# One-bank PSUM tiles for the feed-forward part, in a pool that opens where the pool of the attention's score tiles closes

## The chip, the cores and the metric

The kernel runs on one core of a Trainium2 chip, as one program in one launch. The metric is the time of an execution in microseconds of the device; where several executions are given, their median stands for the kernel. A profile comes from one execution, and its times count from the first instruction of that execution.

## The reference

The reference computes attention and then two feed-forward layers, all in float32.

- Attention: two batches of eight heads, 576 positions, 64 columns a head. q and k are rotated by position, the scores are softmax(q k^T / 8), and the result is the scores times v.
- The result is laid out as 1152 tokens of 512 columns, x.
- First layer: h = max(x w_in, 0) with 2048 columns, and y = (h * h) w_out, 512 columns.
- Second layer: a = y w_a and b = y w_b with 1536 columns each, and the output is (a * b) w2_out, 1152 x 512.

## The kernel before, in words

**How it is ordered.** The body of the kernel doesn't issue instructions as it goes. It describes operations to a planner (class `Plan`): which engines may run each, how long it is taken to last, which operations it follows, which buffers it takes (`acq`) and which it gives back (`rel`). `Plan.order` plays that forward in time and gives one list, and `Plan.run` then calls the operations' functions in the order of the list. For TensorE (PE), ScalarE (ACT), VectorE (DVE) and GpSimd (POOL) the framework keeps that order on each engine (`manual_schedule` at the end of the kernel function); SyncE (SP), which issues the DMAs, isn't in that list of engines. Which semaphore waits an instruction gets is not in the kernel's text: the framework works them out from the tiles that an instruction reads and writes.

**PSUM.** PSUM has eight banks of 512 float32 columns. One pool, `ps`, holds all of it in six tags: `s0` and `s1` of two banks each, and `t0`, `t1`, `u0`, `u1` of one bank each.

- In the attention, a score tile (`scores`, lines 334 to 370) is a tile of shape [128, 2, 512] on `s0` or `s1`. PE writes the two halves of a row of scores into its two banks, and DVE reads both banks at once (line 364) to negate them and take the row's extreme; ACT then takes the exponential. Transposes go to `t0`/`t1`, products with v and the sums' spreading to `u0`/`u1`.
- In the feed-forward part the planner knows six banks by name, `m0` to `m5` (`BANKS`, line 260). `m0` to `m3` are the two halves of two tiles of shape [128, 2, 512] on `s0` and `s1` (`SM`, line 258); `m4` and `m5` are one-bank tiles on `u0` and `u1` (`TM`, line 259; they appear as `mu` in the profile, the other four as `m`). `t0` and `t1` serve the conversion of weights there. Each of these feed-forward tiles is made when it is first used and stays to the end.
- The planner gives each bank out by itself: `bank` (line 513) asks for any of the six, takes the one that is free first, and the operation that reads it last gives it back. The four halves come free in the plan when the last scores are through.

**The feed-forward part.** The numbers are split into a high and a low part, so a product of two matrices takes three matmuls (`three`, lines 606 to 609: high by high, high by low, low by high).

- `unit1` (line 628): one block of 128 columns of h for 384 tokens, 12 matmuls of 384 columns into one bank. ACT takes the maximum with zero out of the bank (line 645), DVE multiplies that by the bank once more (line 646), then ACT and POOL or DVE split the square into its two parts (lines 520 and 517).
- `out1` (line 660): 12 matmuls into one bank, which ACT copies or DVE adds into an accumulator in SBUF (`yacc`, lines 654 and 655).
- `split_y`: the accumulated y is split, and sums and differences of its blocks are made for the second layer, which multiplies 2 x 2 blocks by seven products instead of eight.
- `super2` (line 728): seven products, each six matmuls of 288 columns, into three banks called al, be and gm; ACT copies out of them (lines 760, 764, 768), DVE adds and multiplies out of them (lines 772, 776, 781, 785).
- `out2` (line 799): six matmuls of 512 columns into one bank, which DVE adds into the output's accumulator (`oacc`, line 655); the last round's sums go to HBM by DMA (line 834).
- `convert` and `two_parts` turn weights, loaded as 8-byte numbers, into the two parts; ACT, DVE and POOL share that work, and it runs beside the matmuls all through the feed-forward part, until about 540 us.

In time, the last scores are written at about 147 us, the first `unit1` starts at 157.5 us, the second layer at about 360 us, and the last matmul ends at about 578 us.

Of the kernel before, what the change touches and what calls it, by code (L numbers as in the profile page):

```python
# [7 lines left out]
F32 = mybir.dt.float32  # L8
# [8 lines left out]
P = 128  # L17
# [14 lines left out]
NS = 2  # L32
# [189 lines left out]
def attention_moe_moe2_kernel(ctx: ExitStack, tc: tile.TileContext, qk, rope, vm, vt, ident_in, sel_in, w_in, w_out, w_a, w_b, w2_out, out):  # L222
# [3 lines left out]
    sb = ctx.enter_context(tc.tile_pool(name="sb", bufs=1))  # L226
    st_p = ctx.enter_context(tc.tile_pool(name="st", bufs=3))
    ps = ctx.enter_context(tc.tile_pool(name="ps", bufs=1, space=bass.MemoryType.PSUM))

    xall = sb.tile([P, 2, KC, NTB * TB], F32R, tag="x", name="x")  # L230
    CR = sb.tile([P, 2, 2, S], F32, tag="g2", name="cs_rot")
# [15 lines left out]
    def lazy(make):  # L247
        got = []

        def get():  # L250
            if not got:
                got.append(make())
            return got[0]
        return get

    WB = lazy(lambda: sb.tile([P, NWB, 2, DM], F32R, tag="wb", name="w_b"))
    STAGS, TTAGS, UTAGS = tuple(f"s{k}" for k in range(NS)), ("t0", "t1"), ("u0", "u1")
    SM = [lazy(lambda k=k: ps.tile([P, 2, 512], F32, tag=f"s{k}", name=f"m{k}")) for k in range(NS)]
    TM = [lazy(lambda t=t: ps.tile([P, 512], F32, tag=t, name=f"m{t}")) for t in UTAGS]
    BANKS = {f"m{k}": (lambda k=k: SM[k // 2]()[:, k % 2]) if k < 2 * NS else TM[k - 2 * NS] for k in range(2 * NS + 2)}  # L260
    MTAGS = tuple(BANKS)
    WTAGS = ("wa",) + tuple(f"wb{k}" for k in range(NWB))
    pl = Plan({
# [15 lines left out]
    def half(h):  # L279
        return slice(64 * h, 64 * h + 64)  # L280
# [31 lines left out]
    def rotate(p):  # L312
        b, rot = XA[p], ROT[p % 2]
        done = load_qk_done[p]
        war = [SDONE[p - 2, 4]] if p > 1 else []
        r = {}

        def x():
            return b()

        if p:
            for qi in (1, 0):
                m = pl.op("POOL", ("s", 2 * S), lambda e, qi=qi: e.tensor_tensor(out=x()[:, :, qi, :], in0=x()[:, :, qi, :], in1=cs, op=ALU.mult), [done[qi, 0]])  # L323
                r[qi] = pl.op("POOL", ("s", S), lambda e, qi=qi: e.tensor_tensor(out=rot[:, qi, :], in0=x()[:, 0, qi, :], in1=x()[:, 1, qi, :], op=ALU.add), [m] + war)
            r[2] = r[0]
        else:
            for key, qi, c in ((1, 1, slice(0, S)), (0, 0, slice(0, QS)), (2, 0, slice(QS, S))):
                w = c.stop - c.start
                m = [pl.op(FLEX, ("s", w), lambda e, n=n, qi=qi, c=c: e.tensor_tensor(out=x()[:, n, qi, c], in0=x()[:, n, qi, c], in1=cs[:, n, c], op=ALU.mult), [done[1, n] if qi else done[0, c.start]] + done[1, n].k0[:n + 1]) for n in range(2)]
                r[key] = pl.op(FLEX, ("s", w), lambda e, qi=qi, c=c: e.tensor_tensor(out=rot[:, qi, c], in0=x()[:, 0, qi, c], in1=x()[:, 1, qi, c], op=ALU.add), m)  # L330
        pl.op(None, None, None, list(r.values()), rel=[b])
        ROPE[p] = r

    def scores(p, c):
        rot = ROT[p % 2]
        if c == 0:
            rotate(p)
            ST[p] = lazy(lambda: st_p.tile([P, 2, 9], F32, tag="st", name=f"st{p}"))
        r = ROPE[p]
        tail = c == 4  # L340
        s = [Buf(STAGS, {t: (lambda t=t, h=h: ps.tile([P, 2, 512], F32, tag=t, name=f"s{p}_{c}_{h}")) for t in STAGS}) for h in range(1 if tail else 2)]
        SB[p, c] = s
        pr = Buf("P", None)
        pr.k = len(EXP) % NP
        st = ST[p]

        def mm(e):
            k0 = [rot[half(h), 1, :] for h in range(2)]
            if tail:
                q0 = (rot[half(0), 0, 512:576], rot[half(1), 0, 0:64])  # L350
                for h, bk, c0, kk, n in ((0, 0, 0, 0, 288), (1, 1, 0, 352, 224), (1, 1, 224, 0, 64), (0, 1, 0, 288, 288), (1, 0, 0, 64, 288)):
                    pe.matmul(s[0]()[half(h), bk, c0:c0 + n], q0[h], k0[h][:, kk:kk + n], start=True, stop=True, skip_group_check=True)  # L352
            else:
                for bk in range(2):
                    for h in range(2):
                        q0 = rot[half(h), 0, 64 * h + c * P:64 * h + (c + 1) * P]
                        pe.matmul(s[h]()[:, bk, 0:288], q0, k0[h][:, bk * 288:bk * 288 + 288], start=True, stop=True)  # L357

        o = pl.op("PE", ("us", 1.15), mm, [r[1], r[0]] + ([r[2]] if c else []), acq=s)
        SDONE[p, c] = o  # L360
        ex = []
        for h in range(len(s)):
            j = 2 * c + h
            m = pl.op("DVE", ("us", 0.85), lambda e, h=h, j=j: e.tensor_scalar(  # L364
                out=PP[:, pr.k, h, :].rearrange("p (b n) -> p b n", b=2), in0=s[h]()[:, :, 0:288], scalar1=-1.0, scalar2=None,
                op0=ALU.mult, op1=ALU.min, accum_out=st()[:, 0, j:j + 1]), [o], acq=[pr] if h == 0 else [], rel=[s[h]])
            x = pl.op("ACT", ("us", 0.86), lambda e, h=h, j=j: e.activation(  # L367
                PP[:, pr.k, h, :], PP[:, pr.k, h, :], AF.Exp,
                bias=st()[:, 0, j:j + 1], scale=-1.0, accum_out=st()[:, 1, j:j + 1]), [m])
            ex.append(x)  # L370
        EXP[p, c] = (pr, ex)
# [141 lines left out]
    def bank(name, width):  # L513
        return Buf(MTAGS, {t: (lambda f=f: f()[:, 0:width]) for t, f in BANKS.items()})

# [340 lines left out]
    fixed.append(dma(54, lambda e: e.dma_start(out=sel32, in_=sel_in)))  # L856
    zeros += [pl.op("POOL", ("us", 0.2), lambda e, t=t: e.memset(t, 0.0)) for t in VT]
    scores(0, 0)
    for n, (p, c) in enumerate(order):
        if n + 1 < len(order):  # L860
            scores(*order[n + 1])
        if c == 0:
            load_v(p)
        if c == 1 and 0 < p < NPAIR - 1:
            load_qk_done[p + 1] = load_qk(p + 1)
        if c == 4:
            if p:
                flip(p - 1)
            turned(p, c, 0)
            if p:  # L870
                spread(p - 1, 0)
            turned(p, c, 1)
            if p:
                spread(p - 1, 1)
            recip(p)
        else:
            turned(p, c, 0)
            turned(p, c, 1)
            if p:
                times_v(p - 1, c // 2, c % 2)  # L880
            if c == 3:
                turned(p, c, 2)
        if (p, c) == GATE:
            for k in range(3):
                wide.append(pl.op("DVE", ("us", 0.06), lambda e, k=k: e.memset(sb.tile([P, DM], I64, tag="raw", bufs=3, name=f"later{k}").bitcast(I32)[:, 0:1], 0), EXP[p, c][1]))
    p = NPAIR - 1
# [129 lines left out]
```

## Time and profile before

| what | value |
|---|---|
| median of 3 executions | 583.15 us (583.06 to 583.92) |
| the profiled execution | 583.75 us |
| its span, first to last instruction | 582.0 us |
| PE busy | 562.5 us (97%), 3554 matmuls |
| PE's weight loads | 486.7 us (84%) |
| DVE busy | 395.2 us (68%) |
| ACT busy | 326.9 us (56%) |
| POOL busy | 306.9 us (53%) |
| DMA | 51.16 MB, 88 GB/s on the mean |
| granted TensorE clock | 1.00 on the mean over the span |

The table is the profile's first page. Busy time is the time in which an engine had an instruction of its own under way. PE's matmuls are pipelined, so that one begins while the one before still drains: a matmul of 384 columns is shown with 0.33 us, though the next starts 0.17 us after it. An engine's idle time is listed with what ended it, the releaser: the instruction whose semaphore was the last to let the waiting one go. Tiles are named without their numbers: `m` is any of the four halves, `mu` either of the two one-bank tiles. A row of a timeline gives start, duration, engine, line, operation, out<-in, and in brackets the engine's idle time just before it with its releaser.

### The profile page before, as it was taken

What the parts mean: (1) busy time and instruction counts of PE and PEld (TensorE: products, weight loads), DVE (VectorE), ACT (ScalarE), POOL (GpSimd) and SP (SyncE); (2) the same over time, 40 slices, a digit from 0 to 9 for tenths busy, and PEclk for the clock granted to TensorE, in tenths of its full rate; (3) what the DMA queues carried; (4) which work ended last, traced back from release to release, by engine and by line L of the source; (5) the groups of instructions that cost most, each with busy time, mean ns of one, the idle gap of its engine ahead of it and who ended that gap; (6) DMA issues with size and microseconds to landing.
All of it is one profiled execution on the core that took longest, in us unless ns stands there. A gap on an engine that the chain in (4) does not pass through costs nothing.

```text
span 582.0 us, 9472 instructions
## 1 busy us (share of the span) xinstructions
PE 562.5 (97%) x3554; PEld 486.7 (84%) x3554; DVE 395.2 (68%) x748; ACT 326.9 (56%) x690; POOL 306.9 (53%) x260
## 2 busy tenths in 40 slices
PE   3999999999999999999999999999999999999997
PEld 2666666666699999999999999899988988988986
DVE  3646777776378736836764768987887877886454
ACT  1668888887478657705732545467753654534210
POOL 4598765421377505804761366776656666655000
PEclk9999999999999999999999999999999999999999
DMA  8326242120124423403330210213341322300004
GB/s 280 137 82 211 103 174 94 57 74 21 37 82 138 144 70 112 142 3 109 110 102 8 73 37 1 63 59 134 109 144 42 106 72 73 127 20 1 1 1 163
DMA packets 16018, 51.16 MB, mean 88 GB/s; under 512 B 2889, under 2 KB 3785, under 8 KB 15076
## 3 DMA queue, kind: packets, MB, share of 16 engines
q1 hardware_dynamic: 15972, 50.55, 25.7%
q8 instruction: 28, 0.46, 0.3%
q14 instruction: 18, 0.15, 0.1%
HBM read 48.19 MB, written 2.36 MB: 87 GB/s over the span
## 4 chain that ended last, share of the span: by engine, by line
PE 87%; DVE 7%; POOL 1%; ACT 1%; issue 1%; DMA 1%; SPq 0%; DVEq 0%; POOLq 0%; ACTq 0%
PE m L607 13%; PE m L609 12%; PE m L608 12%; PE s L357 7%; PE t L378 6%; PE av L436 6%; PE mu L607 5%; PE mu L608 5%; PE mu L609 5%; PE m L814 3%; PE m L816 2%; PE m L815 2%; PE av L438 2%; DVE oacc L655 1%; PE s L352 1%; PE mu L816 1%
## 5 line engine op out<-in xcount | busy, mean ns | idle before, releaser
L364 DVE TENSOR_SCALAR_CACHE_REDUCE P<-s 128x576 f32<-128x576 f32 x72 | 52.3, 755 | 32.7 <-PE s L357 24.5
L517 POOL TENSOR_TENSOR g<-v,g 128x384 fp32r<-128x384 f32 (+1 forms) x39 | 46.7, 1199 | 47.0 <-ACT g L520 46.8
L367 ACT ACTIVATE P<-P,st 128x576 f32<-128x576 f32 x72 | 55.5, 775 | 11.9 <-DVE P L364 11.9
L520 ACT CAST g<-v 128x384 fp32r<-128x384 f32 (+1 forms) x72 | 40.6, 566 | 28.2 <-DVE v L785 18.1
L607 PE MATMUL m<-y,w_p 128*128 128x288 f32 x160 | 48.1, 301 | 2.8 <-DVE v L772 1.8
L608 PE MATMUL m<-y,w_p 128*128 128x288 f32 x160 | 47.2, 295 | 0.0
L609 PE MATMUL m<-y,w_p 128*128 128x288 f32 x160 | 47.1, 294 | 0.0
L378 PEld LDWEIGHTS t<-small,P 128*128 128x128 f32 x288 | 31.4, 143 | 14.6 <-issue 10.6
L378 PE MATMUL t<-small,P 128*128 128x128 f32 x288 | 41.3, 285 | 0.0
L323 POOL TENSOR_TENSOR X<-X,cs_rot 128x1152 f32<-128x1152 f32 x14 | 36.7, 2635 | 1.1 <-DMA small<-in_sel 1.1
L607 PEld LDWEIGHTS m<-y,w_p 128*128 128x128 f32 x160 | 30.0, 187 | 6.4 <-DVE oacc L655 2.7
L607 PE MATMUL m<-x,w_i 128*128 128x384 f32 x100 | 33.7, 337 | 0.7 <-DVE v L646 0.5
L357 PE MATMUL s<-cs_rot 64*128 64x288 f32 x128 | 24.5, 484 | 9.8 <-POOL cs_rot L330 8.8
L609 PE MATMUL m<-x,w_i 128*128 128x384 f32 x100 | 33.4, 334 | 0.0
L608 PE MATMUL m<-x,w_i 128*128 128x384 f32 x100 | 33.4, 334 | 0.0
L760 ACT COPY v<-m 128x288 f32<-128x288 f32 x19 | 7.6, 400 | 42.0 <-PE m L609 26.7
L608 PEld LDWEIGHTS m<-y,w_p 128*128 128x128 f32 x160 | 30.1, 188 | 1.1
L517 POOL TENSOR_TENSOR w_i<-bits_i,w_i 128x512 fp32r<-128x512 f32 x8 | 10.3, 1282 | 39.2 <-ACT w_i L520 39.2
L609 PEld LDWEIGHTS m<-y,w_p 128*128 128x128 f32 x160 | 30.0, 188 | 0.0
L655 DVE TENSOR_TENSOR oacc<-m,oacc 128x512 f32<-128x512 f32 (+1 forms) x31 | 20.8, 678 | 12.7 <-PE m L816 7.7
L655 DVE TENSOR_TENSOR yacc<-m,yacc 128x384 f32<-128x384 f32 (+1 forms) x26 | 13.4, 517 | 22.9 <-PE m L609 22.6
L517 DVE TENSOR_TENSOR g<-v,g 128x384 fp32r<-128x384 f32 (+1 forms) x33 | 23.6, 716 | 7.8 <-ACT g L520 7.7
(248 smaller groups left out, 1918.1 us busy)
## 6 DMA issues: line engine op xcount, KB each, us to landing
raw_i<-in_w_in SPq DMA_DIRECT2D x16, 512.0 KB, 3.3
raw_o<-in_w_out SPq DMA_DIRECT2D x16, 512.0 KB, 3.2
X<-in_qk SPq DMA_DIRECT2D x7, 1152.0 KB, 5.3
raw_a<-in_w_a SPq DMA_DIRECT2D x12, 512.0 KB, 3.3
raw_b<-in_w_b SPq DMA_DIRECT2D x12, 512.0 KB, 3.2
raw<-in_w_out SPq DMA_DIRECT2D x12, 512.0 KB, 3.3
V<-in_vm SPq DMA_DIRECT2D x8, 256.0 KB, 5.6
out<-oacc SPq DMA_DIRECT2D x8, 256.0 KB, 2.0
```

The lines of the kernel that those rows point to most:

```text
L323: m = pl.op("POOL", ("s", 2 * S), lambda e, qi=qi: e.tensor_tensor(out=x()[:, :, qi, :], in0=x()[:, :, qi, :], in1=cs, op=ALU.mult), [done ...
L357: pe.matmul(s[h]()[:, bk, 0:288], q0, k0[h][:, bk * 288:bk * 288 + 288], start=True, stop=True)
L364: m = pl.op("DVE", ("us", 0.85), lambda e, h=h, j=j: e.tensor_scalar(out=PP[:, pr.k, h, :].rearrange("p (b n) -> p b n", b=2), in0=s[h]()[ ...
L367: x = pl.op("ACT", ("us", 0.86), lambda e, h=h, j=j: e.activation(PP[:, pr.k, h, :], PP[:, pr.k, h, :], AF.Exp, bias=st()[:, 0, j:j + 1], ...
L378: pe.transpose(b()[0:src.shape[1], k * P:k * P + P] if w is None else b()[0:w, k * P:k * P + P], src, ident)
L436: pe.matmul(b()[half(h), 0:288], v[:, h, k, :], pt[:, h, k, q], start=(k == 0), stop=False, skip_group_check=True)
L517: e.tensor_tensor(out=out_, in0=a, in1=b, op=ALU.subtract)
L520: h = pl.op("ACT", ("s", n), lambda e: e.copy(hi_(), val()), after)
L607: pe.matmul(dst, wh, mh, start=first, stop=False, skip_group_check=open_)
L608: pe.matmul(dst, wh, ml, start=False, stop=False, skip_group_check=open_)
L609: pe.matmul(dst, wl, mh, start=False, stop=last, skip_group_check=open_)
L655: return pl.op("DVE", ("p", width), lambda e: e.tensor_tensor(out=acc(), in0=dst(), in1=acc(), op=ALU.add), [o] + b.prior, rel=[b])
```

## The change

The pool of the score tiles becomes a pool of its own, `wide_ps`, which is opened by hand behind `ps`. The score tiles are taken from it. When the first of `m0` to `m3` is used, the function `narrow` closes that pool and opens another, `narrow_ps`, and the four banks become four tiles of shape [128, 512] in it, in place of the halves of two tiles. The planner's names, its buffers, costs and dependencies are what they were.

```diff
     ps = ctx.enter_context(tc.tile_pool(name="ps", bufs=1, space=bass.MemoryType.PSUM))
+    wide_ps = tc.tile_pool(name="wide_ps", bufs=1, space=bass.MemoryType.PSUM)
+    sps = wide_ps.__enter__()
...
-    SM = [lazy(lambda k=k: ps.tile([P, 2, 512], F32, tag=f"s{k}", name=f"m{k}")) for k in range(NS)]
+
+    def narrow():
+        wide_ps.__exit__(None, None, None)
+        return ctx.enter_context(tc.tile_pool(name="narrow_ps", bufs=1, space=bass.MemoryType.PSUM))
+
+    mps = lazy(narrow)
+    SM = [lazy(lambda k=k: mps().tile([P, 512], F32, tag=f"m{k}", name=f"m{k}")) for k in range(2 * NS)]
     TM = [lazy(lambda t=t: ps.tile([P, 512], F32, tag=t, name=f"m{t}")) for t in UTAGS]
-    BANKS = {f"m{k}": (lambda k=k: SM[k // 2]()[:, k % 2]) if k < 2 * NS else TM[k - 2 * NS] for k in range(2 * NS + 2)}
+    BANKS = {f"m{k}": SM[k] if k < 2 * NS else TM[k - 2 * NS] for k in range(2 * NS + 2)}
...
-        s = [Buf(STAGS, {t: (lambda t=t, h=h: ps.tile([P, 2, 512], F32, tag=t, name=f"s{p}_{c}_{h}")) for t in STAGS}) for h in range(1 if tail else 2)]
+        s = [Buf(STAGS, {t: (lambda t=t, h=h: sps.tile([P, 2, 512], F32, tag=t, name=f"s{p}_{c}_{h}")) for t in STAGS}) for h in range(1 if tail else 2)]
```

## Rows read from the trace of the kernel before

**Rows 1.** Busy time by stretch: us, then busy us of the engines, clock, DMA:
```profile
366.00:566.00 200.00, 195.11 (x1236) 179.06 (x1236) 148.99 (x269) 98.98 (x203) 110.07 (x83) 1.00 0.21 69
```

**Rows 2.** Waits of PE from 157 us on: us in total, times, longest:
```profile
PE m L607 <- DVE v L772: 1.8, 2, 1.4
PE m L607 <- DVE oacc L655: 1.0, 4, 0.3
PE m L814 <- DVE oacc L655: 0.8, 1, 0.8
PE mu L607 <- DVE v L781: 0.7, 1, 0.7
PE m L607 <- DVE v L646: 0.5, 1, 0.5
PE m L814 <- DVE v L785: 0.3, 1, 0.3
PE m L607 <- ACT v L645: 0.2, 1, 0.2
PE m L607 <- ACT v L760: 0.2, 1, 0.2
```

**Rows 3.** Timeline of PE, first matmuls of the first units of the feed-forward part:
```profile
157.54 0.45 PE L607 MATMUL m<-x,w_i 128*128 128x384 f32 x1
...
160.57 0.44 PE L607 MATMUL m<-x,w_i 128*128 128x384 f32 x1 [0.24 <-ACT v L645]
...
164.83 0.33 PE L607 MATMUL m<-x,w_i 128*128 128x384 f32 x1
...
166.91 0.33 PE L607 MATMUL mu<-x,w_i 128*128 128x384 f32 x1
...
168.99 0.33 PE L607 MATMUL mu<-x,w_i 128*128 128x384 f32 x1
```

**Rows 4.** Timeline of ACT, two reads of those units' banks:
```profile
167.17 0.49 ACT L645 ACTIVATE v<-m 128x384 f32<-128x384 f32 x1 [2.06 <-PE m L609]
...
170.50 0.49 ACT L645 ACTIVATE v<-mu 128x384 f32<-128x384 f32 x1
```

**Rows 5.** Timeline of DVE, its last read of a score tile:
```profile
147.09 0.76 DVE L364 TENSOR_SCALAR_CACHE_REDUCE P<-s 128x576 f32<-128x576 f32 x1 [1.83 <-PE s L352]
```

**Rows 6.** Timeline of PE, a wait with idle time and the matmul behind it:
```profile
238.47 0.44 PE L607 MATMUL m<-x,w_i 128*128 128x384 f32 x1 [0.46 <-DVE v L646]
238.75 0.33 PE L608 MATMUL m<-x,w_i 128*128 128x384 f32 x1
```

**Rows 7.** Timeline of PE, a late start without idle time:
```profile
356.40 0.29 PE L609 MATMUL m<-g,w_b 128*128 128x288 f32 x1
356.66 0.41 PE L607 MATMUL m<-g,w_o 128*128 128x288 f32 x1
```

**Rows 8.** Timeline of PE, the longest wait and a later group of the same tiles:
```profile
370.50 0.40 PE L607 MATMUL m<-y,w_p 128*128 128x288 f32 x1 [1.42 <-DVE v L772]
...
373.89 0.30 PE L607 MATMUL m<-y,w_p 128*128 128x288 f32 x1
```

**Rows 9.** Timeline of DVE around that wait:
```profile
366.29 1.61 DVE L517 TENSOR_TENSOR y<-gT,y 128x576 fp32r<-128x576 f32 x1
...
371.69 0.44 DVE L776 TENSOR_TENSOR u<-m,u 128x288 f32<-128x288 f32 x1
372.40 0.46 DVE L781 TENSOR_TENSOR v<-m,v 128x288 f32<-128x288 f32 x1 [0.26 <-PE m L609]
```

**Rows 10.** Timeline of DVE, the read that the wait of L814 at 433.84 us names:
```profile
433.09 0.69 DVE L655 TENSOR_TENSOR oacc<-m,oacc 128x512 f32<-128x512 f32 x1 [0.56 <-PE m L609]
```

**Rows 11.** Timeline of DVE, the last additions (the first row merges three):
```profile
576.73 1.62 DVE L655 TENSOR_TENSOR oacc<-m,oacc 128x512 f32<-128x512 f32 x3 [2.03 <-PE m L816]
578.27 0.41 DVE L655 TENSOR_TENSOR oacc<-mu,oacc 128x256 f32<-128x256 f32 x1
```

**Rows 12.** DMA issues of the page: KB each, median us from issue to landing:
```profile
raw_a<-in_w_a SPq DMA_DIRECT2D x12, 512.0 KB, 3.3
```

## The prediction

> **What bounds the kernel now.** I read the page first: PE is busy for 97% of the span, so whatever this change is worth must come out of PE's remaining time or out of the tail. Next the busy time by stretch: in the second layer, 366 to 566 us, PE is busy for 195.1 of 200 us, DVE for 149.0, POOL for 110.1, ACT for 99.0 [rows 1]. PE is the limit there and the others have room; the missing 4.9 us are where to look. The table of waits names them: from the start of the feed-forward part PE sat idle 12 times for a semaphore, 5.5 us in all, nearly always at the first matmul into an `m` tile, and the releaser is an ACT or DVE instruction that reads an `m` tile [rows 2].
>
> Then the question on which all hangs: does that reader read the bank which PE is about to write, or its neighbour in the same two-bank tile? The rows name tiles without numbers. The bank follows from the plan, which hands `m0`, `m1`, `m2`, `m3` out in turn to the first four units. The second unit (into `m1`) starts at 160.57, after 0.24 us of idle time that ended with ACT's read of the first unit's bank `m0` [rows 3]. `m1` had no reader since the scores. The third unit fills `m2` up to 164.83, the fourth `m3` from 164.83 to 166.91 [rows 3]; ACT's read of the third unit starts only at 167.17, after 2.06 us of waiting for a matmul [rows 4]. So it waited for the fourth unit, with which it shares a tile and not a bank. The one-bank tiles behave otherwise: ACT reads the fifth unit's `mu` at 170.50 [rows 4], while the sixth unit (the other `mu`, from 168.99 [rows 3], 2.08 us long) is being written. Reads and writes of one tile are ordered against each other over both of its banks.
>
> I followed this through the whole part by matching the rows to the instructions of the program of before, in order. Of the 12 waits, 10 are for a reader of the neighbouring bank: all but the 0.8 us of L814 for `oacc` and the 0.7 us into `mu` [rows 2]. About fifty reads on ACT and DVE also sat idle until matmuls of the neighbour were through.
>
> **The change part by part.** *Instructions.* No engine's work is added, removed or reordered: the planner sees the same names, costs and dependencies. Only waits differ, so the cost of the edit itself is that of the pools.
>
> *Closing one pool and opening the other.* The first use of the new tiles must follow the last use of the old. DVE's last read of a score tile ends at 147.85 [rows 5]; the first matmul into `m0` starts at 157.54 [rows 3]. Cover: 9.7 us in which PE does other attention work; were that gone, the cost would be the remainder of a 0.76 us read. Were the boundary drawn to everything ahead in PE's queue, it could reach the last copies out of the attention's other banks, at most the 0.4 us by which such a copy outlasts 157.54 (estimate, from the 0.5 us reads of [rows 4]). I take nothing.
>
> *Waits of PE that go.* A wait costs more than its idle time. At 238.47 the idle time is 0.46 us, but a matmul is shown with 0.33 us and the stream runs at one per 0.173 us (12 matmuls from 164.83 to 166.91 [rows 3]), which hides 0.16; and the next follows at 0.28 instead of 0.173 [rows 6]. That is 0.46 + 0.16 + 0.11 = 0.73 us, 0.27 over what is shown. The ten waits have 1.8 + 1.0 + 0.5 + 0.3 + 0.2 + 0.2 = 4.0 us of idle time [rows 2], so 4.0 + 10 x 0.27 = 6.7 us. Five more late starts show no idle time, such as 356.66, 0.26 us behind a matmul whose successor is due after 0.13 [rows 7]; with the slow second matmul that is about 0.25 each, 1.3 us. Together 8.0 us.
>
> *A wait that stays but shrinks.* L814 at 433.84 waits for a reader of its own bank; but that read, at 433.09, itself sat idle 0.56 us for a matmul of the neighbouring bank [rows 10]. 0.56 of it goes.
>
> *The tail.* The addition at 576.73 waited 2.03 us [rows 11], through the following group of six matmuls, which fills the other half of its tile; then three additions run back to back in 1.62 us and the last one, at 578.27, follows them without a pause [rows 11]. Without the false wait the first of them runs over 1 us earlier, the last starts when its own matmuls end (estimate: 0.1 us earlier), and its DMA isn't issued behind three others. I take 0.35 us, bounded by 0 and the 1.62.
>
> *What is late next.* PE arrives earlier, while DVE has its own queue. The longest wait, 370.50, is worth 1.42 + 0.27 = 1.7 us [rows 8]. DVE there runs without a pause from 366.29 to 372.13 [rows 9]; the addition at 372.40 on which the group at 373.89 rests [rows 8, 9] can then start at about 372.05 and end near 372.5, where PE would come at 373.89 - 1.7 = 372.2. So 0.4 of the 1.7 comes back, a quarter. The other removed waits have DVE with pauses near them (a quarter of the stretch is idle [rows 1]), and for each the last reader of the bank that PE really wants was through before PE came. For all of it to come back the next need would have to wait for the same DVE instruction each time (bound: 8.0 lost again); the other end is nothing. By the nearest row, a quarter at the worst place, I take a sixth of the other 6.3 us: 1.05.
>
> *Contention.* ACT and DVE will read a bank while PE writes its neighbour, which one tile didn't allow. The read of `mu` during writes to the other `mu` took 0.49 us, and so did the read of `m` with its neighbour at rest [rows 4]. I take nothing. The Trainium skill (PSUM — Partial Sum Buffer, section PSUM bank collisions raise a hardware error) has engines collide when they share a bank and quadrant and run clean on different banks, which agrees with the 0.49 us on both sides: the order that goes wasn't needed by the chip.
>
> **Sum.** 8.0 + 0.56 + 0.35 - 0.4 - 1.05 = 7.45 us. The profiled execution took 583.75 (span 582.0 and 1.75 around it), 0.6 above the median; off the median of 583.15 it leaves 575.7 us.
>
> **Rivals.**
>
> *Half comes back.* DVE's queue takes the place of the false waits: PE runs into additions that are really needed, as at 373.89. For it: DVE is the busiest engine after PE. Against: it loses its own idle waits too. If half of the 8.0 returns, 583.15 - 4.0 = 579.2.
>
> *The change doesn't do it.* The releaser named is only the last of several; behind the neighbour's reader might stand a wait for weights, or for the planner's six banks themselves. Then the time stays, 583.1. Against: no wait of PE names a weight's conversion [rows 2], and the read at 167.17 had nothing else to wait for. The Trainium skill speaks for this rival (Perfetto Trace Analysis, section Optimization Strategy): gaps that repeat on the engine that should be full can mean too little PSUM for the next tile. By that rule a change that leaves six banks at six would gain nothing; the trace disagrees, since the bank that PE wanted at 160.57 had no reader left.
>
> *Slower: the weights' transfers.* SP's queue isn't kept in the plan's order. If the new waits let it issue weights in another order, a conversion comes a landing late, 3.3 us [rows 12], and PE waits for it in full where that weight had no lead. It decides from the third such place: 583.15 - 7.45 + 3 x 3.3 = 585.6. Against: weights are no releaser of PE anywhere [rows 2], so they have a lead.
>
> **How the numbers follow.** Forecast 0.70, half back 0.20, no effect 0.06, slower 0.04. A measurement of this kernel can tell 0.2%, 1.2 us, from no change. Forecast and half back are both faster by more, with a little lost to smaller gains: faster 0.91; no effect and its neighbours 0.05; slower 0.04. Range: the low end is nothing returned, all 1.07 us of the 433.84 wait gone and the tail's gain, 583.15 - 8.0 - 1.07 - 0.35 = 573.7, rounded down to 573.5; the high end takes in the half-back case at 579.2: 579.5.
>
> **What would show it.** Right: PE's ten waits gone from the table, its idle time from 157 us on near 1.5 us, of which 0.7 is the wait into `mu` at the end (there the last product needs the addition before it, so it stays); ACT's read of the third unit at about 165 instead of 167.17; the read at 433.09 without idle time; the first of the last additions over 1 us earlier. Half back: new waits of PE for DVE L781, L776 or L772 behind 370 us. Pools that cost: idle time before the first `m` matmul at 157.54. Wrong altogether: the same releasers with the same times, or a wait for a weight.

## The result and the profile after

The changed kernel takes 574.7 us, the median of four executions, the kernel before 583.53 us beside it on the same chip (583.06 to 584.51). Three of the four took 573.43 to 574.74 us; the fourth, left out of the ratio, took 1385.88 us at the same granted clock (1.00), a time that no other execution on record comes near and no profile explains. The ratio is 0.9839, 95% interval 0.9816 to 0.9863, and the medians differ by 8.8 us. The forecast was 575.7 us.

The profiled execution took 574.66 us, its span 572.9 us against 582.0, so 9.1 us less. Line numbers after are 8 higher than before from `three` on: L607 is L615, L655 is L663, L781 is L789, L814 is L822.

The page of the changed kernel, the line of busy times and the chain's shares by engine:

```profile
PE 558.0 (97%) x3554; PEld 486.4 (85%) x3554; DVE 397.5 (69%) x748; ACT 328.7 (57%) x690; POOL 306.7 (54%) x260
...
PE 94%; DVE 3%; DMA 1%; ACT 0%; issue 0%; SPq 0%; POOL 0%; DVEq 0%; POOLq 0%
```

The counts are those of before. In the chain, PE had 87% and DVE 7% before: it is above all DVE's part of the path that shrank.

The busy time of the changed kernel in the second layer (us, busy us of PE, PEld, DVE, ACT, POOL, clock, DMA), for [rows 1]:

```profile
366.00:566.00 200.00, 198.97 (x1265) 184.57 (x1264) 154.52 (x274) 99.53 (x200) 107.91 (x82) 1.00 0.22 75
```

PE lacks 1.0 us of the stretch instead of 4.9, and DVE does more in the same time because more of the work falls into it (274 instructions instead of 269).

The waits of PE in the changed kernel from 157 us on, the whole table (us in total, times, longest), for [rows 2]:

```profile
PE mu L615 <- DVE v L789: 0.7, 1, 0.7
PE m L615 <- DVE v L789: 0.2, 1, 0.2
```

Twelve waits have become two, 5.5 us of idle time 0.9, where the forecast had near 1.5. The first is the wait into `mu`, which was there before. The timeline of PE in the changed kernel, for [rows 3, 8] and for that wait:

```profile
157.68 0.44 PE L615 MATMUL m<-x,w_i 128*128 128x384 f32 x1
...
160.36 0.45 PE L615 MATMUL m<-x,w_i 128*128 128x384 f32 x1
...
164.66 0.33 PE L615 MATMUL m<-x,w_i 128*128 128x384 f32 x1
...
166.74 0.33 PE L615 MATMUL mu<-x,w_i 128*128 128x384 f32 x1
...
370.67 0.29 PE L617 MATMUL mu<-y,w_p 128*128 128x288 f32 x1
371.17 0.40 PE L615 MATMUL m<-y,w_p 128*128 128x288 f32 x1 [0.21 <-DVE v L789]
371.40 0.29 PE L616 MATMUL m<-y,w_p 128*128 128x288 f32 x1
...
429.73 0.50 PE L822 MATMUL m<-w,g 128*128 128x512 f32 x1
...
556.22 0.40 PE L615 MATMUL mu<-y,w_p 128*128 128x288 f32 x1 [0.68 <-DVE v L789]
```

The first unit starts where it did (157.68 against 157.54) and without idle time, the second one without a wait. At 371.17 the product starts 0.50 us after the matmul ahead, where 0.13 is usual, and the one behind it at 0.23 instead of 0.13. This is the place at which the forecast had 0.4 us come back.

The readers of the changed kernel, first ACT's read of the third unit, for [rows 4]:

```profile
165.00 0.48 ACT L653 ACTIVATE v<-m 128x384 f32<-128x384 f32 x1
```

and DVE's for [rows 9 to 11] (566.85 is the first of the last four additions, the row at 568.21 merges two):

```profile
370.67 0.44 DVE L789 TENSOR_TENSOR v<-m,v 128x288 f32<-128x288 f32 x1
...
428.99 0.68 DVE L663 TENSOR_TENSOR oacc<-m,oacc 128x512 f32<-128x512 f32 x1
...
566.85 0.69 DVE L663 TENSOR_TENSOR oacc<-m,oacc 128x512 f32<-128x512 f32 x1 [0.67 <-PE m L824]
568.21 1.14 DVE L663 TENSOR_TENSOR oacc<-m,oacc 128x512 f32<-128x512 f32 x2 [0.67 <-PE m L824]
569.64 0.42 DVE L663 TENSOR_TENSOR oacc<-mu,oacc 128x256 f32<-128x256 f32 x1 [0.29 <-PE mu L824]
```

ACT reads the third unit at 165.00 instead of 167.17, while PE fills the fourth unit's bank (164.66 to 166.74), and in the same time (0.48 us). The Trainium skill (PSUM — Partial Sum Buffer, section PSUM bank collisions raise a hardware error) has different banks run clean beside each other; this row agrees. The addition at 428.99 has lost its 0.56 us of idle time. The first of the last four additions, which had waited 2.03 us [rows 11], now starts 2.47 us ahead of the last matmul (569.32) instead of 1.11 (576.73 against 577.85), and the last one waits for its own matmuls alone.

**The sum by the trace.** For every matmul of the feed-forward part I took the distance from the start of the one ahead, less the usual distance behind a matmul of that width (the median: 0.173 us at 384 columns, 0.133 at 288, 0.234 at 512, 0.120 at 256); what is left is its late start. Those of over 0.06 us add up to 10.2 us before and 2.1 us after, 8.1 less. This sum leaves out one of the ten waits, that at 160.57 [rows 3], because small matmuls of the attention stand just ahead of it; the same place takes 0.31 us less after. From the first `m` matmul to the start of the last matmul it is 420.3 us before and 411.6 after, 8.7 less, so under 0.3 us came from late starts smaller than 0.06. From the start of the last matmul to the end of the span it is 4.1 us before and 3.5 after, 0.6 less. The start at 157.68 is 0.1 later. 8.7 + 0.6 - 0.1 = 9.2, against 9.1 by the spans.

### The profile page after: what moved, and what is told of

The parts are those of the page before. It is cut to its first block, busy times and chain, and to the rows that moved or that the text cites. A ratio compares the mean times of both kernels' runs of the same rounds, so it can differ in the third digit from the quotient of the medians.

```text
span 572.9 us, 9468 instructions
## 1 busy us (share of the span) xinstructions
PE 558.0 (97%) x3554; PEld 486.4 (85%) x3554; DVE 397.5 (69%) x748; ACT 328.7 (57%) x690; POOL 306.7 (54%) x260
## 4 chain that ended last, share of the span: by engine, by line
PE 94%; DVE 3%; DMA 1%; ACT 0%; issue 0%; SPq 0%; POOL 0%; DVEq 0%; POOLq 0%
PE m L615 13%; PE m L617 13%; PE m L616 13%; PE s L365 8%; PE t L386 6%; PE av L444 6%; PE mu L615 6%; PE mu L617 6%; PE mu L616 6%; PE m L822 3%; PE m L824 3%; PE m L823 3%; PE av L446 2%; PE mu L824 2%; PE mu L823 2%; PE mu L822 2%
## 5 line engine op out<-in xcount | busy, mean ns | idle before, releaser
L615 PE MATMUL m<-y,w_p 128*128 128x288 f32 x160 | 47.2, 295 | 0.2 <-DVE v L789 0.2
L365 PE MATMUL s<-cs_rot 64*128 64x288 f32 x128 | 24.1, 477 | 10.3 <-POOL cs_rot L338 9.4
L615 PE MATMUL m<-x,w_i 128*128 128x384 f32 x100 | 33.6, 336 | 0.0
L525 POOL TENSOR_TENSOR w_i<-bits_i,w_i 128x512 fp32r<-128x512 f32 x8 | 10.3, 1287 | 40.6 <-ACT w_i L528 40.6
L615 PEld LDWEIGHTS m<-y,w_p 128*128 128x128 f32 x160 | 30.0, 188 | 1.6 <-DVE v L789 0.4
L663 DVE TENSOR_TENSOR yacc<-m,yacc 128x384 f32<-128x384 f32 (+1 forms) x26 | 13.4, 517 | 22.6 <-PE m L617 22.4
L663 DVE TENSOR_TENSOR oacc<-m,oacc 128x512 f32<-128x512 f32 (+1 forms) x31 | 21.0, 679 | 10.5 <-PE m L824 10.2
```

Source lines behind the costliest of these rows:

```text
L525: e.tensor_tensor(out=out_, in0=a, in1=b, op=ALU.subtract)
L615: pe.matmul(dst, wh, mh, start=first, stop=False, skip_group_check=open_)
L663: return pl.op("DVE", ("p", width), lambda e: e.tensor_tensor(out=acc(), in0=dst(), in1=acc(), op=ALU.add), [o] + b.prior, rel=[b])
```

## The experiments

Each kernel is the changed one with the edit shown. "Length" is the time from the first `m` matmul to the start of the last matmul; it leaves out the attention, after which the part begins at 156.8 to 158.4 us from one profile to the next.

| kernel | median us | ratio to before | length us | late starts us (without that at the second unit) |
|---|---|---|---|---|
| before | 583.5 | | 420.3 | 10.2 |
| changed | 574.7 | 0.9839 [0.9816, 0.9863] | 411.6 | 2.1 |
| e1 pools, two-bank tiles | 583.74 | 0.9998 [0.9985, 1.0011] | 420.3 | 10.3 |
| e2 first tile split | 578.50 | 0.9914 [0.9898, 0.9931] | 414.6 | 4.9 |
| e3 second tile split | 578.31 | 0.9913 [0.9898, 0.9928] | 415.8 | 5.9 |
| e4 one four-bank tile | 674.71 | 1.1572 [1.1531, 1.1612] | 512.6 | 102.6 |
| e5 other partners | 583.55 | 1.0001 [0.9992, 1.0010] | 420.6 | 11.0 |
| e6 last products reordered | 573.72 | 0.9829 [0.9816, 0.9843] | 410.7 | 1.2 |
| e7 more DVE load | 574.37 | 0.9845 [0.9831, 0.9858] | 412.1 | 2.6 |
| changed, again | 574.46 | 0.9845 [0.9832, 0.9859] | 411.7 | 2.1 |

e1 to e4 ran on one chip together, with 583.86 us for the kernel before; e5 to e7 and the changed kernel again ran together, with 583.42.

**e1: the pools alone.** Pool closed and pool opened as in the change, tiles of two banks as before.

```diff
-    SM = [lazy(lambda k=k: mps().tile([P, 512], ...)) for k in range(2 * NS)]
+    SM = [lazy(lambda k=k: mps().tile([P, 2, 512], ...)) for k in range(NS)]
...
-    BANKS = {f"m{k}": SM[k] if k < 2 * NS else ...}
+    BANKS = {f"m{k}": (lambda k=k: SM[k // 2]()[:, k % 2]) if k < 2 * NS else ...}
```

> The pools of the change (one closes, one opens at the first m bank) with the feed-forward tiles as they were, two tiles of two banks. If the gain comes from ordering over a tile's two banks: no gain, ratio to before 0.998 to 1.002 (about 583.5 us), with PE's ten waits for a neighbouring bank back and at most 0.4 us for the pool boundary. If it comes from the pools or from where in PSUM the tiles now lie: ratio 0.984 (about 574.7 us).

Measured: 583.74 us, no change. The waits of PE in e1 (as above):

```profile
PE m L615 <- DVE v L780: 1.8, 2, 1.4
PE m L615 <- DVE oacc L663: 1.0, 4, 0.4
PE m L822 <- DVE oacc L663: 0.8, 1, 0.8
```

These are the first rows of [rows 2] but for a tenth. The pools and the place in PSUM do nothing; the size of the tile does it all. The Trainium skill (Perfetto Trace Analysis, section Optimization Strategy) says that gaps that repeat on the engine that should be full can mean too little SBUF or PSUM for the next tile, by the count of buffers or the size of tiles; here e1 and the changed kernel have the same six banks and differ by 9 us.

**e2 and e3: one tile split, the other not.** In e2 `m0` and `m1` have a bank each and `m2`, `m3` share a tile, in e3 the other way round. The shared tile is called `mw` in the profile, lines are 9 above those of before.

```diff
+    TWO = lazy(lambda: mps().tile([P, 2, 512], F32, tag="w", name="mw"))
...
-    BANKS = {f"m{k}": SM[k] if k < 2 * NS else TM[k - 2 * NS] ...}
+    BANKS = {f"m{k}": TM[k - 2 * NS] if k >= 2 * NS else SM[k] if k in (0, 1) else (lambda k=k: TWO()[:, k % 2]) ...}    # e2; (2, 3) in e3
```

> m0 and m1 become one-bank tiles, m2 and m3 stay halves of a two-bank tile. Twelve of the late starts of PE that wait for a neighbour in the trace of before are in the tile of m0 and m1; start to start they add to 6.8 us (370.50 alone 1.7). Tile theory: ratio 0.987 to 0.989, 576.3 to 577.3 us, with PE still waiting in the second tile near 445 and 556 us of before. Pool theory: 0.984.

> m2 and m3 become one-bank tiles, m0 and m1 stay halves of a two-bank tile. In the second tile are three late starts worth 1.2 us together, 0.6 us of the wait at 433.84, and the addition of the tail that waits for its neighbour (0.3 to 0.5 us). Tile theory: ratio 0.995 to 0.998, 580.8 to 582.3 us, with the wait of 1.4 us at 370.50 still there. Pool theory: 0.984.

Measured: 578.50 and 578.31 us. Both miss what was expected: splitting the first tile gives 5.0 us by its ratio (0.86% of 583.86), less than expected, and splitting the second 5.1 (0.87%), far more. By lengths it is 5.7 and 4.5 us, 10.2 together, where both at once give 8.7. The waits of PE, e2:

```profile
PE mw L616 <- DVE v L781: 1.3, 1, 1.3
PE mw L823 <- DVE oacc L664: 0.8, 1, 0.8
PE mu L616 <- DVE v L790: 0.7, 1, 0.7
PE mw L616 <- DVE v L655: 0.3, 1, 0.3
```

and e3 (two smaller rows left out):

```profile
PE mw L616 <- DVE v L781: 1.4, 1, 1.4
PE mu L616 <- DVE v L790: 0.7, 1, 0.7
PE mw L616 <- DVE oacc L664: 0.6, 2, 0.5
...
```

Two things show. In e2 the longest wait of [rows 8] isn't gone but has moved by one product to the tile that is still shared: the two tiles had waits in store one behind the other, and only the first was on show. And waits vanished from the tile that wasn't split: in e3 those at 238.47, 468.11, 487.24 and 524.88 of the kernel before, in e2 that at 445.01, where the expectation still had one. (One grew: that at 521.87, from 0.30 us of idle time to 0.47 in e3.) The one at 468.11 in the timelines of DVE and PE of the kernel before:

```profile
463.39 0.69 DVE L655 TENSOR_TENSOR oacc<-m,oacc 128x512 f32<-128x512 f32 x1 [0.83 <-PE m L609]
...
467.37 0.68 DVE L655 TENSOR_TENSOR oacc<-m,oacc 128x512 f32<-128x512 f32 x1
```

```profile
467.63 0.29 PE L609 MATMUL mu<-y,w_p 128*128 128x288 f32 x1
468.11 0.40 PE L607 MATMUL m<-y,w_p 128*128 128x288 f32 x1 [0.18 <-DVE oacc L655]
```

and the same instructions in e3:

```profile
459.64 0.69 DVE L664 TENSOR_TENSOR oacc<-m,oacc 128x512 f32<-128x512 f32 x1
...
463.89 0.68 DVE L664 TENSOR_TENSOR oacc<-mw,oacc 128x512 f32<-128x512 f32 x1
```

```profile
464.67 0.29 PE L618 MATMUL mu<-y,w_p 128*128 128x288 f32 x1
464.81 0.30 PE L616 MATMUL mw<-y,w_p 128*128 128x288 f32 x1
```

Before, DVE sits idle 0.83 us ahead of 463.39 for a matmul into the neighbouring bank of the second tile, and from there runs without a pause up to the read at 467.37. That read ends at 468.05, while PE would come at 467.76 (0.13 behind 467.63), so PE waits. With the second tile split the first of the two reads starts without idle time at 459.64; the second ends at 464.57, and PE comes at 464.81 without a wait. Measured from the last `mu` matmul, DVE's second read starts 0.26 us ahead before and 0.78 us ahead in e3. So at this place a false wait of a reader delays DVE's queue, and that makes a wait of PE for the other tile. The forecast counted PE's waits one by one; they hang together through DVE.

**e4: one tile for all four.**

```diff
+    ALL4 = lazy(lambda: mps().tile([P, 4, 512], F32, tag="w", name="m0"))
...
+    BANKS = {f"m{k}": (lambda k=k: ALL4()[:, k]) if k < 2 * NS else TM[k - 2 * NS] ...}
```

> All four banks m0 to m3 are slices of one tile of [128, 4, 512]: each bank has three neighbours in its tile in place of one. Tile theory: slower than before, at least the 10 us of late starts once more, 593 to 615 us (ratio 1.015 to 1.055), with PE waiting for ACT and DVE at many first matmuls of a group. Pool theory: 0.984 as after the change.

Measured: 674.71 us, the direction expected, the size far above it. The three largest waits of PE in e4:

```profile
PE m L615 <- DVE v L654: 16.4, 13, 1.7
PE m L615 <- DVE oacc L663: 8.1, 11, 1.2
PE m L615 <- DVE yacc L663: 8.0, 13, 0.7
```

Banks and plan are the same, and PE's late starts are 102.6 us. From two banks in a tile to four the loss grows from 9 to 100 us. With four, a unit that follows another into the tile waits for that one's reader; with two, the plan's turn through the banks mostly leaves the neighbour time to be read (this reading is argued from the order of the banks, the sizes are measured).

**e5: two-bank tiles with other partners.** `m0` shares with `m2` and `m1` with `m3`.

```diff
+    BANKS = {f"m{k}": (lambda k=k: SM[k % 2]()[:, k // 2]) if k < 2 * NS else ...}    # SM as in e1
```

> The change's pools, but again two tiles of two banks, with other partners than before: m0 shares a tile with m2 and m1 with m3 (before: m0 with m1, m2 with m3). Names, order and number of banks are the same. Theory (a whole tile is ordered, whatever bank is read): late starts sit where the partner's reader is late, not where it was before. The second unit, into m1, has then no partner that was used, so its late start of before at 160.57 (0.24 us) goes; units into m0 and m2 get them in their place. Neighbours that are used two units apart are nearer to being done, so some of the readers' waits are shorter: 576 to 583 us, anything but the times of e1 to the row. Rival (which physical bank pairs lie side by side, not the tile, sets the waits): the waits stay at the same units as before, 160.57 among them, and the time is 583.5 to 584.

Measured: 583.55 us, a little above the theory's range and inside the rival's, so the time doesn't decide. The places do. The waits of PE in e5, the four largest:

```profile
PE mu L615 <- DVE v L789: 1.2, 2, 0.7
PE m L615 <- DVE v L654: 1.1, 1, 1.1
PE m L615 <- DVE v L789: 1.0, 1, 1.0
PE mu L822 <- DVE u L784: 0.9, 1, 0.9
```

and the second and fourth unit in its timeline of PE:

```profile
160.31 0.45 PE L615 MATMUL m<-x,w_i 128*128 128x384 f32 x1
...
164.43 0.34 PE L617 MATMUL m<-x,w_i 128*128 128x384 f32 x1
165.88 0.45 PE L615 MATMUL m<-x,w_i 128*128 128x384 f32 x1 [1.11 <-DVE v L654]
```

The second unit's wait of [rows 3] is gone, since `m1` shares with nothing used, and the fourth unit, into `m3`, waits 1.11 us for DVE's read of the second, in `m1`. Even `mu` gets two new waits, though no tile of its own changed: DVE comes late to it. These are ten waits in other places, and nothing in them makes their sum that of e1; I take the equal total for chance.

**e6: the last products reordered.** The product that starts late at 556.22 is the last of its group (not the fourth, as the expectation says). It fills the `mu` bank out of which DVE has to add product 5 first. The edit lets products 4 and 5 change places, so that product 4, into an `m` bank, stands between product 5 and the last one; the last one keeps its place.

```diff
-            out_ += body[:2] + ([end] if end else []) + body[2:]
+            rest = body[2:] if (body, last) != supers[-1] else [body[2], body[3], body[5], body[4]]
+            out_ += body[:2] + ([end] if end else []) + rest
```

> The changed kernel with the order of the last five products altered in the last group of units: the fourth product, which fills mu and at 556.22 starts 0.84 us late (and its next matmul 0.10) for a DVE addition, is put one product later, so that another product covers that addition. Theory (the remaining 0.94 us is a true dependency and can be covered by PE work that waits for nothing): that late start goes or falls under 0.3 us, the span falls by 0.6 to 0.9, 573.8 to 574.1 us. Rival (the products behind need the same additions, so that the wait moves to the next of them): 574.5 to 575, with a late start of about 0.8 at another product. Other rival: the last addition comes later in the tail because the product that now stands last has a longer way to the output: 574.8 to 575.5.

Measured: 573.72 us, 0.1 below the theory's range. All of PE's waits that are left in e6, and the product that waited at 556.22:

```profile
PE m L615 <- DVE v L789: 0.2, 1, 0.2
```

```profile
555.30 0.32 PE L615 MATMUL mu<-y,w_p 128*128 128x288 f32 x1
```

The length falls from 411.7 to 410.7 us, close to the 0.94 us of the two late starts. e6 has the lowest median of all, but its ratio's interval overlaps that of the changed kernel; that it is the faster one rests on the length in the trace.

**e7: more work for DVE.** One scratch write more in each of 24 groups. It waits for product 5 and nothing waits for it, so the planner places it: in the trace 11 of the 24 stand behind an addition, the others behind other work, and none between product 5 and the addition that reads it.

```diff
+    LOAD = lazy(lambda: sb.tile([P, 384], I32, tag="load", name="load"))
...
+            pl.op("DVE", None, lambda e: e.memset(LOAD(), 0), [o])
```

> The changed kernel with one more DVE instruction (a memset of 128x384 in a scratch tile) in each of the 24 groups of units, behind an addition; everything else in the same order. At the 0.2 to 0.45 us which DVE's instructions of that width take in the trace this is 5 to 11 us of load on the engine that stands between PE's products. Theory (released from the false waits, DVE has so much slack that lateness dies out in it): few of the 24 show at PE, 574.6 to 575.6 us. Rival (a sixth to a quarter of any lateness of DVE comes back at PE, as the prediction took it): one sixth to one quarter of 5 to 11 us, 575.6 to 577.5 us.

Measured: 574.37 us, the theory's side. The added group among DVE's groups in e7 (busy us, mean ns, idle before), the stretch of [rows 1], and the only wait of PE that the changed kernel doesn't have:

```profile
L791 DVE MEMSET load<- 128x384 int32 x24 | 9.1, 378 | 1.2
```

```profile
366.00:566.00 200.00, 198.82 (x1261) 184.10 (x1260) 162.12 (x297) 99.69 (x200) 107.12 (x82) 1.00 0.23 76
```

```profile
374.10 0.40 PE L617 MATMUL m<-y,w_b 128*128 128x288 f32 x1 [0.15 <-ACT u L778]
```

DVE is given 9.1 us more and the length grows by 0.4 us, nearly all at 374.10 (0.32 us, and 0.11 at the next matmul), just behind the stretch in which DVE had no pause before either [rows 9]. Of this load a twentieth shows at PE. That isn't the same as a twentieth of any lateness: behind ten of the 24 writes DVE still has 0.37 to 2.13 us of idle time, so they fell into pauses, and no run puts work between a product and its addition.

**The changed kernel again.**

> The changed kernel once more, beside the other three on the same chip, as what they are compared with: 574.7 us, ratio to the kernel before 0.983 to 0.985, and the same three late starts above 0.4 us (371.17, 429.73, 556.22).

Measured: 574.46 us, ratio 0.9845, and the three late starts at 370.30, 428.86 and 555.36 us (this execution entered the part 0.85 us earlier) with 0.36, 0.30 and 0.84 us, each with 0.10 more at the next matmul: 0.47, 0.40 and 0.95.

## Why the prediction was right

- **That the readers named in PE's waits read the neighbour's bank**: shown. e1 keeps pools and banks and all waits stay; the change takes them; e5 moves them to the other partner.
- **The pools at nothing**: right, 157.68 against 157.54, and e1 at 0.9998.
- **8.0 us of false waits, 0.56 us at L814, 0.4 us come back at the worst place**: nearly right, 8.0 us measured against 8.16 together. Matched place by place, matmul for matmul, the ten waits gave 6.5 us (6.7 forecast) and the five late starts without idle time 1.3 (as forecast). At L814 the late start fell from 1.05 to 0.40 us, 0.64. At 371.17 0.47 us came back, through the addition the forecast named (L781 before, L789 after).
- **A sixth of the other 6.3 us, 1.05 us, comes back**: the term that was wrong. At no place but 371.17 does a matmul start over 0.05 us later behind the one ahead than before; only the true waits of the table are left. The place at 370.50, where DVE runs without a pause, was the worst and not a measure for the rest. Moreover the readers were freed as well, which the forecast held against the rival of half coming back and then left out of this term: e3 shows that it makes PE's waits vanish where nothing was changed for PE, and e7 that DVE takes 9 us more of work at the price of 0.4.
- **What the forecast didn't count**: 0.7 us, of which 0.4 in four late starts of 0.1 us that had stood alone, the rest in smaller ones.
- **The tail at 0.35 us**: 0.6. The last addition ends 0.1 us earlier behind the last matmul, as forecast, and from its end to the span's end it is 2.8 us instead of 3.3, which the forecast put down to its transfer not being issued behind three others. The issue of that transfer begins 0.28 us after the addition's end before and 0.03 after, which agrees for half of it. The same 2.8 us show in e3 and e5, where the last additions don't wait for a neighbour either, and 3.3 in e1 and e2, where they do.

These make the gap: 1.05 + 0.7 + 0.25 (tail) - 0.2 (false waits) - 0.1 (later start) = 1.7 us more than the 7.45 forecast, the 9.1 by the spans. By the medians the gain is 8.8 us, 1.4 more than forecast. That the time itself is only 1.0 us off is chance for the other 0.4: the kernel before took 583.53 us beside the changed one, and the forecast counted from 583.15.

The rivals: half coming back needed new waits for DVE L781, L776 or L772, of which there is one of 0.2 us. No effect is refuted by the waits that went. The transfers of weights in another order didn't happen: on each engine, SP among them, the instructions of both programs stand in the same order.

What stays open: the share of each reader's false wait in what PE lost wasn't measured one by one; the rows of e3 show the chain at one place of four. What work put between a product and its addition would cost wasn't tried.

## What to carry over

When PE waits for a reader, find out which bank that reader has, not only which tile: the profile names tiles, the plan names banks, and a tile of two banks given out by halves is ordered as one. Where false waits hold both the writer and its readers, taking them away frees both queues. Here time came back only at the one place where the reader's queue was full, so charge such a place, and no other without a reason of its own. And split the tiles all at once: half the split may only move the longest wait to the tile that is left.

## What the runs showed that was not expected

- The step from two to four banks in a tile costs ten times the step from one to two: 674.71 us against 583.74 and 574.7.
- The feed-forward part repeats almost exactly: 420.30 and 420.29 us in the kernel before and e1, 411.64 and 411.67 in two profiles of the changed kernel, while its beginning moves by 1.6 us between profiles. Gains under 1 us are read better from such a length than from the span.
